# Hidden activations of one token tile kept on chip instead of passing through DRAM, in a fused attention and FFN kernel

## The chip, the core and the metric

The kernel runs on one core of a Trainium2 chip. The metric is the device time of one execution in microseconds, the median of several runs. Engines are named as in the profile: PE multiplies matrices (PEld loads its stationary operand), DVE and ACT work on vectors, POOL is the third such engine, SP issues the DMAs.

## The reference

Windowed attention over 8 x 8 heads of 576 tokens, 64 wide, then a gated feed-forward network over the 4608 tokens. All data are float32.

```
scores = q @ k^T / 8, kept where 0 <= i - j < 64
attn   = softmax(scores) @ v                  # (8, 8, 576, 64)
x      = attn, heads side by side             # (4608, 512)
out    = (sigmoid(x @ w_gate) * (x @ w_val)) @ w_out     # 512 -> 1536 -> 512
```

## The kernel before

**Tiles.** The 4608 tokens are cut into 12 tiles of TT = 384, worked off in pairs (tiles 0 and 1 are the first pair). The attention of a tile consists of four units (t, p), each two heads: scores `s` on PE (L219), softmax on DVE and ACT (L243 to L268), transposes `pp` on PE (L300), their copies `pT` on ACT (L305), the products `oo` on PE (L329), and a copy `xf` out of PSUM on ACT (L317), which makes its bank free for the next unit's scores.

**The FFN of the first pair** is done plainly. The 1536 hidden columns are NF = 12 blocks j of 128. `up` (L360) makes the gate's and the value's products of a block, `gate_table` (L369) the sigmoid, `up_val` their product `h32` (L388), and `hidden_split` (L377) splits it into a high part `hh` (L380) and a rest `hl` (L382), since a product is made of three matmuls: high by high, high by rest, rest by high. `down` (L416) multiplies these with w_out and sums over j in the PSUM tiles `y`; after the last j, ACT copies `y` to `yo` (L419), and SP stores it (L420). Tile 0 runs `down` right behind its `up`. Tile 1 runs `down` only after all blocks of both tiles are made; its blocks 0 to 9 go out to the DRAM tensor `hd` by `put_hidden` (L395, L396) and come back by `get_hidden` (L403) as `hb`; the last KEEP = 2 blocks stay in the ring of `hh` and `hl`. The later pairs run another scheme with sums and differences (products `pr`, `y` at L612), from 200 us on.

**What runs beside it.** The weights arrive as 64-bit floats and are converted in the first 190 us, 36 tiles `m_j` of 128 x 512 (m: gate, value, output): ACT makes `w32` (L117) and `raw` (L118) from a loaded tile, DVE combines them (L126, L128, L130), ACT casts the high part `w` (L157), DVE makes the rest (L158), SP stores all of it for the later pairs. Between these stand the attention units of tiles 2 and 3, and from 170 us on the preparation of the second pair: `x_prep` (L590: differences t1 and xf, L566, L567, L574) and `x_part`, `x_rest` (x_T, x_B; L602, L607), and sums of weights `ws` (L546 on ACT, L548 on DVE).

**Memory.** A tile gets a slot by its tag; several tiles with one tag take the slots in turn, and a new tile waits until the last reader of the old one is done. x0 to x13 hold the split inputs, x10 to x13 first the v of units (0,2) to (1,1); e0 to e4 are for hidden tiles of later pairs; the tag `raw` has RAW = 6 slots, the tag `w32` W32 = 3 (the conversion's w32, then yo and t1).

**Order.** Each step is put into a list `events` with a time written by hand; the list is sorted, and the steps are issued in that order to a scheduler which simulates the engines and decides in which order DVE, ACT, POOL and SP run their instructions. PE keeps the order of the program. On the chip each engine runs its instructions strictly in the order decided.

Of the kernel before, what the change touches and what calls it, by code (L numbers as in the profile page):

```python
# [9 lines left out]
F32 = mybir.dt.float32  # L10
F32R = mybir.dt.float32r
# [7 lines left out]
P = 128  # L19
BLK = 64  # L20
TT = 384
# [5 lines left out]
def attn_ffn(ctx: ExitStack, tc: tile.TileContext, qT, kT, vN, w_gate, w_val, w_out, out, outT):  # L27
# [3 lines left out]
    nc = tc.nc  # L31
# [3 lines left out]
    NF = w_gate.shape[0]  # L35
# [10 lines left out]
    RAW, W32 = 6, 3  # L46
# [3 lines left out]
    xp = ctx.enter_context(tc.tile_pool(name="xp", bufs=1))  # L50
    mp = ctx.enter_context(tc.tile_pool(name="mp", bufs=2))
    ap = ctx.enter_context(tc.tile_pool(name="ap", bufs=1))
    sm = ctx.enter_context(tc.tile_pool(name="sm", bufs=8))
    dr = ctx.enter_context(tc.tile_pool(name="dr", bufs=1, space=bass.MemoryType.DRAM))
# [286 lines left out]

    hh = {}
    yb = {}
    hd = dr.tile([NF, P, 2, TT], F32, name="hd")
    nbank = [-1]

    def h_bank(nm):
# [27 lines left out]
        gate_table(t, j, up(t, j, 0))  # L375

    def hidden_split(t, j, h32, eng):  # L377
        h_hi = mp.tile([P, TT], F32R, name=f"hh_{t}_{j}", tag="hh", bufs=3)
        h_lo = mp.tile([P, TT], F32R, name=f"hl_{t}_{j}", tag="hl", bufs=3)
        nc.vector.tensor_copy(out=h_hi, in_=h32)  # L380
        hh[(t, j)] = (h_hi, h_lo)
        return eng.tensor_sub(out=h_lo, in0=h32, in1=h_hi.bitcast(F32))  # L382

    def up_val(t, j):
        ph = up(t, j, 1)
        g = gates.pop((t, j))
        h32 = mp.tile([P, TT], F32, name=f"h32_{t}_{j}", tag="c", bufs=CB)
        nc.vector.tensor_mul(out=h32, in0=ph, in1=g)  # L388
        last = hidden_split(t, j, h32, nc.vector)
        if t == 0:  # L390
            marks[j] = (chain[-1], last.ins)

    def put_hidden(t, j):
        h_hi, h_lo = hh.pop((t, j))
        nc.sync.dma_start(out=hd[j, :, 0, :], in_=h_hi.bitcast(F32))  # L395
        nc.sync.dma_start(out=hd[j, :, 1, :], in_=h_lo.bitcast(F32))  # L396

    def get_hidden(t, j):
        if j > 5:
            hb = xp.tile([P, 2, TT], F32R, name=f"hb_{t}_{j}", tag=f"x{10 + (j + 2) % 4}")  # L400
        else:
            hb = mp.tile([P, 2, TT], F32R, name=f"hb_{t}_{j}", tag="raw", bufs=RAW)
        nc.sync.dma_start(out=hb.bitcast(F32), in_=hd[j])  # L403
        hh[(t, j)] = (hb[:, 0, :], hb[:, 1, :])


    def down(t, j, i, first, last):
        h_hi, h_lo = hh[(t, j)]
# [369 lines left out]
    UPT, DNT, PRT = 4.2, 2.1, 1.05  # L778
    events = []

    def put(tm, o, f, *a):
        events.append((tm, o, f, a))

    KEEP = 2
    AHEAD = 2
    DPT = DNT / TB
    APT = (0.9, 0.8, 0.9, 1.5, 0)
# [11 lines left out]
    for n in range(2 * NP):  # L799
        t, p = divmod(n, NP)  # L800
# [17 lines left out]
    at, now = {}, 0.0  # L818
# [5 lines left out]
    def attend(i):  # L824
        nonlocal now
        for f, t, p, *done in fill.get(i, ()):
            if f in (0, 3):
                put(now - LOAD_AHEAD, 8, load_qk, t, p)
                put(now - LOAD_AHEAD, 8.5, load_v, t, p)
            put(now, 6, stages[f], t, p, *done)  # L830
            now += APT[f]

    for i, (kind, t, j) in enumerate(plan):
        attend(i)
        at[(kind, t, j)] = now
        if (kind, t, j) == ("up", 0, 0):
            now = -9.9
        if kind == "up":
            put(now, 9, up_gate, t, j)
            now += UPT / 2  # L840
            attend(i + 0.5)
            put(now, 9, up_val, t, j)
            if t == 1 and j < NF - KEEP:
                put(now, 9.1, put_hidden, t, j)
            now += UPT / 2
        else:
            for x in range(TB):
                put(now + x * DPT, 9, down, t, j, x, j == 0, j == NF - 1)
            now += DNT
        if (kind, t, j) == ("up", 0, 0):  # L850
            now = 0.0
    for i in range(KINDS * NF):
        j, m = divmod(i, KINDS)
# [10 lines left out]
    fill[46] = [(3, *unit(2, 0))]  # L864
    fill[47] = [(4, *unit(2, 0))]

    def last_tile(t, js, ready):


        nonlocal now  # L870
        items = [(j, x) for x in range(TB) for j in js[:2]] + [(j, x) for j in js[2:-2] for x in range(TB)]
        items += [(j, x) for x in range(TB) for j in js[-2:]]
        for n, j in enumerate(js):
            put(now + n * DNT - ready[0], 9.4, ready[1], t, j)
        for n, (j, x) in enumerate(items):
            if n % TB == 0 and t == 1:
                attend(len(plan) + n // TB)
                attend(len(plan) + n // TB + 0.5)
            put(now, 9, down, t, j, x, j == js[0], j == js[-1])
            now += DPT  # L880

    last_tile(1, list(range(NF)), (7, lambda t, j: j < NF - KEEP and get_hidden(t, j)))

# [99 lines left out]
    for _, _, f, a in events:  # L985
        if f in (conv_a, conv_b, conv_c):
            with ExitStack() as behind:
                j, m = divmod(a[0], KINDS)
# [56 lines left out]
```

## Time and profile before

| | us |
|---|---|
| median of 3 runs | 970.04 (968.94 to 970.25) |
| the profiled execution | 968.12 |
| its span in the trace | 966.3 |
| PE busy | 946.8 (98%) |
| DVE busy | 692.8 (72%) |
| ACT busy | 597.3 (62%) |
| granted clock of PE | 1.0 |

The span is the time from the first to the last recorded instruction of the profiled execution; 1.8 us lie around it. In the lines of the profile, a name before the arrow is what an instruction writes, behind it what it reads, numbers left out; a bracket at a timeline row's end gives the idle time ahead of the instruction and what ended it. Times within the span are counted from its start.

### The profile page before, as it was taken

How to read it: one execution, taken by the hardware profiler on the slowest of the kernel's cores; microseconds unless marked ns; L12 is line 12 of the kernel's file. 1: busy time of each engine (PE TensorE's matmuls, PEld its weight loads, DVE VectorE, ACT ScalarE, POOL GpSimd, SP SyncE). 2: the span in 40 equal slices, each digit the busy share in tenths (PEclk: the TensorE clock that was granted, in tenths of full speed). 3: DMA queues.
4: the chain of work that ended last, by engine and by line, in shares of the span. 5: the costliest groups of instructions: out<-in, count | busy, mean ns of one | idle time of the engine just before them, and what ended most of it. 6: DMA issues, size and time to landing. Idle time of an engine off the chain costs nothing.

```text
span 966.3 us, 20552 instructions
## 1 busy us (share of the span) xinstructions
PE 946.8 (98%) x7200; PEld 904.1 (94%) x7200; DVE 692.8 (72%) x1873; ACT 597.3 (62%) x1479; POOL 141.8 (15%) x232
## 2 busy tenths in 40 slices
PE   6899999999999999999999999999999999999998
PEld 4798999889999999999999999999999999999998
DVE  7889989756776964666876666796566697567782
ACT  7888877647787644666754666664666675222350
POOL 4200103327661000110100111100110100000000
PEclk9999999999999999999999999999999999999999
DMA  9899999948998868889989888878888868988464
GB/s 344 313 384 356 398 353 346 395 165 290 319 305 283 287 205 265 279 259 323 342 265 301 285 257 271 262 258 284 293 264 259 262 212 263 306 252 257 142 211 160
DMA packets 110838, 272.41 MB, mean 282 GB/s; under 512 B 12048, under 2 KB 42896, under 8 KB 110736
## 3 DMA queue, kind: packets, MB, share of 16 engines
q1 hardware_dynamic: 110736, 271.11, 83.2%
q8 instruction: 57, 0.93, 0.4%
q14 instruction: 45, 0.37, 0.1%
HBM read 214.17 MB, written 56.89 MB: 280 GB/s over the span
## 4 chain that ended last, share of the span: by engine, by line
PE 82%; ACT 6%; DVE 5%; DMA 3%; issue 2%; POOL 1%; SPq 0%; DVEq 0%; ACTq 0%
PE pr L612 39%; PE y L612 23%; PE ph L360 6%; PE y L416 4%; PE s L219 3%; PE pp L300 2%; PE s L329 2%; ACT p L251 2%; DMA a<-w32d 1%; DMA w32d<-w 1%; PE oo L329 1%; ACT L251 1%; ACT pT L305 1%; PE pr L329 1%; ACT L369 1%
## 5 line engine op out<-in xcount | busy, mean ns | idle before, releaser
L612 PE MATMUL pr<-x_T,wt 128*128 128x384 f32 x1224 | 227.9, 338 | 0.0
L612 PEld LDWEIGHTS pr<-x_T,wt 128*128 128x128 f32 x1224 | 211.3, 188 | 4.2 <-issue 2.6
L612 PE MATMUL pr<-x_B,wt 128*128 128x384 f32 x1008 | 187.5, 336 | 0.0
L612 PE MATMUL y<-h,wot 128*128 128x384 f32 x1008 | 176.0, 334 | 0.0
L612 PEld LDWEIGHTS pr<-x_B,wt 128*128 128x128 f32 x1008 | 175.0, 188 | 0.6 <-DMA wt<-wd 0.3
L612 PEld LDWEIGHTS y<-h,wot 128*128 128x128 f32 x1008 | 174.6, 188 | 0.5 <-DVE h L655 0.3
L268 POOL TENSOR_TENSOR p<-p,rs 128x384 f32<-128x384 f32 x76 | 66.4, 888 | 567.5 <-DVE rs L259 511.2
L720 ACT CAST h<-h 128x384 fp32r<-128x384 f32 x168 | 82.6, 515 | 67.2 <-PE y L612 34.4
L251 ACT ACTIVATE p<-p,mn 128x128 f32<-128x128 f32 x288 | 111.0, 394 | 6.2 <-DVE mn L243 5.6
L360 PE MATMUL ph<-x,w 128*128 128x384 f32 x576 | 106.2, 338 | 0.1
L721 DVE TENSOR_TENSOR h<-h,h 128x384 fp32r<-128x384 f32 x168 | 88.6, 553 | 24.1 <-ACT h L720 22.7
L360 PEld LDWEIGHTS ph<-x,w 128*128 128x128 f32 x576 | 99.7, 188 | 2.4 <-issue 0.9
L243 DVE CUSTOM_DVE_ANT_0 p<-s,m 128x128 f32<-128x128 f32 x288 | 65.7, 286 | 38.8 <-PE s L219 38.5
L369 ACT ACTIVATE g<-c 128x384 f32<-128x384 f32 x90 | 46.6, 524 | 69.1 <-DVE c L651 68.8
L655 DVE TENSOR_TENSOR h<-c,g 128x384 f32<-128x384 f32 x90 | 55.9, 621 | 29.8 <-ACT g L369 25.5
L369 ACT ACT_TABLE_LOAD x40 | 51.3, 1283 | 13.4 <-DVE c L651 12.8
L305 ACT COPY pT<-pp 128x384 f32<-128x384 f32 x96 | 41.4, 480 | 28.2 <-PE pp L300 28.1
L219 PE MATMUL s<-k,q 64*64 64x128 f32 x1152 | 46.0, 287 | 7.7 <-DMA k<-in_kT_dram 4.9
L622 DVE TENSOR_TENSOR c<-pr,p 128x384 f32<-128x384 f32 x60 | 33.1, 551 | 27.7 <-PE pr L612 27.7
L251 ACT ACT_TABLE_LOAD x39 | 50.0, 1283 | 0.7
L251 ACT ACTIVATION_READ_ACCUMULATOR p<-p,mn 128x1 f32 x264 | 49.9, 189 | 0.0
L219 PEld LDWEIGHTS s<-k,q 64*64 64x64 f32 x1152 | 33.4, 138 | 14.3 <-DMA q<-in_qT_dram 5.2
(113 smaller groups left out, 1326.8 us busy)
## 6 DMA issues: line engine op xcount, KB each, us to landing
wt<-wd SPq DMA_DIRECT2D x186, 512.0 KB, 4.5
wot<-wod SPq DMA_DIRECT2D x84, 512.0 KB, 4.4
v<-in_vN_dram SPq DMA_DIRECT2D x48, 384.0 KB, 5.2
wd<-ws SPq DMA_DIRECT2D x48, 256.0 KB, 4.7
k<-in_kT_dram SPq DMA_DIRECT2D x48, 224.0 KB, 5.2
q<-in_qT_dram SPq DMA_DIRECT2D x48, 192.0 KB, 5.0
w32d<-w SPq DMA_DIRECT2D x36, 256.0 KB, 5.2
wd<-w SPq DMA_DIRECT2D x36, 256.0 KB, 5.6
```

Source lines behind the costliest of these rows:

```text
L219: pe(nc.tensor.matmul(sc[h][half * BLK:(half + 1) * BLK, u, :], qt[h * BLK:(h + 1) * BLK, U * BLK:(U + 1) * BLK], kt[h * BLK:(h + 1) * BLK ...
L243: nc.vector.tensor_tensor_reduce(out=pt[:, u, :], in0=sc[:, u, :], in1=masks[key], op0=ALU.add, op1=ALU.min, scale=-SCALE, scalar=3.0e38, ...
L251: exp = nc.scalar.activation(pt[:, u, :], pt[:, u, :], AF.Exp, bias=mn[:, u:u + 1], scale=-1.0, **sums)
L268: eng.tensor_mul(out=pt, in0=pt, in1=rs.unsqueeze(2).broadcast_to([P, UP, P]))
L305: cp = nc.scalar.copy(pT, pp)
L329: pe(nc.tensor.matmul(oo[U // 2][h * BLK:(h + 1) * BLK, U % 2 * BLK:(U % 2 + 1) * BLK], vt[:, U, h * BLK:(h + 1) * BLK], pT[h][:, U // 2, ...
L360: pe(nc.tensor.matmul(ph, l, r, start=i == 0, stop=i == len(prs) - 1))
L369: act = nc.scalar.activation(g, c, AF.Sigmoid)
L612: pe(nc.tensor.matmul(ps, l, r, start=first and i == 0, stop=last and i == 2, skip_group_check=not check))
L655: nc.vector.tensor_mul(out=hidden(s, k)[2 * r + b], in0=c, in1=gates.pop((t, j)))
L720: nc.scalar.copy(h2[:, 0, :], src)
L721: nc.vector.tensor_sub(out=h2[:, 1, :], in0=src, in1=h2[:, 0, :].bitcast(F32))
```

## The change

The ten blocks j = 0 to 9 of tile 1 are split directly into tiles `h2_1_j` that keep both parts: blocks 0 to 3 in the slots x10 to x13, 4 to 8 in e0 to e4, 9 in one slot of `raw`. `down` reads them there. `put_hidden`, `get_hidden`, the DRAM tensor `hd` and their events are gone.

```diff
-    hd = dr.tile([NF, P, 2, TT], F32, name="hd")
+    KEEP = 2
...
     def hidden_split(t, j, h32, eng):
-        h_hi = mp.tile([P, TT], F32R, name=f"hh_{t}_{j}", tag="hh", bufs=3)
-        h_lo = mp.tile([P, TT], F32R, name=f"hl_{t}_{j}", tag="hl", bufs=3)
+        if t == 1 and j < NF - KEEP:
+            pool, tag, bufs = (xp, f"x{10 + j}", 1) if j < 4 else (xp, f"e{j - 4}", 1) if j < 9 else (mp, "raw", RAW)
+            h2 = pool.tile([P, 2, TT], F32R, name=f"h2_{t}_{j}", tag=tag, bufs=bufs)
+            h_hi, h_lo = h2[:, 0, :], h2[:, 1, :]
+        else:
+            h_hi = mp.tile([P, TT], F32R, name=f"hh_{t}_{j}", tag="hh", bufs=3)
+            h_lo = mp.tile([P, TT], F32R, name=f"hl_{t}_{j}", tag="hl", bufs=3)
         nc.vector.tensor_copy(out=h_hi, in_=h32)
...
-    def put_hidden(t, j):
-        h_hi, h_lo = hh.pop((t, j))
-        nc.sync.dma_start(out=hd[j, :, 0, :], in_=h_hi.bitcast(F32))
-        nc.sync.dma_start(out=hd[j, :, 1, :], in_=h_lo.bitcast(F32))
-
-    def get_hidden(t, j):
-        if j > 5:
-            hb = xp.tile([P, 2, TT], F32R, name=f"hb_{t}_{j}", tag=f"x{10 + (j + 2) % 4}")
-        else:
-            hb = mp.tile([P, 2, TT], F32R, name=f"hb_{t}_{j}", tag="raw", bufs=RAW)
-        nc.sync.dma_start(out=hb.bitcast(F32), in_=hd[j])
-        hh[(t, j)] = (hb[:, 0, :], hb[:, 1, :])
...
-            if t == 1 and j < NF - KEEP:
-                put(now, 9.1, put_hidden, t, j)
...
-    def last_tile(t, js, ready):
+    def last_tile(t, js):
...
-        for n, j in enumerate(js):
-            put(now + n * DNT - ready[0], 9.4, ready[1], t, j)
...
-    last_tile(1, list(range(NF)), (7, lambda t, j: j < NF - KEEP and get_hidden(t, j)))
+    last_tile(1, list(range(NF)))
```

PE's order is the same but for names. With 30 DMAs less in its simulation, the scheduler orders DVE and ACT anew between about 50 and 212 us. In the kernel after, lines of `hidden_split` and `up_val` have numbers higher by 5, and those behind them lower by 9 (L557 for L566). Three places follow; each row is an instruction with its line, its output, its input and the output's size, and the last number of a name is a running number of the tile.

The first place is on ACT at 73 us, around the copy `xf_2_0` that frees the bank for the scores of unit (2,2). Before:

```order
L305 COPY pT1_2_0_1241<-pp1_2_0_1237 128x384
L117 ACTIVATE w32_1_4_1258<-raw_1_4_1182 128x512
L369 ACTIVATE g_0_3_1256<-ph0_0_3_1243 128x384
L118 ACTIVATE raw_0_5_1363<-raw_0_5_1363 128x512
L157 CAST w0_4_1265<-w32_0_4_1228 128x2x256
L118 ACTIVATE raw_1_5_1374<-raw_1_5_1374 128x512
L317 COPY xf_2_0_1316<-oo_2_0_1303 128x384
L157 CAST w1_4_1297<-w32_1_4_1258 128x2x256
L117 ACTIVATE w32_2_3_1271<-raw_2_3_1199 128x512
L118 ACTIVATE raw_2_4_1391<-raw_2_4_1391 128x512
```

The same stretch of ACT after:

```order
L305 COPY pT1_2_0_1231<-pp1_2_0_1227 128x384
L157 CAST w0_4_1255<-w32_0_4_1218 128x2x256
L369 ACTIVATE g_0_3_1246<-ph0_0_3_1233 128x384
L118 ACTIVATE raw_0_5_1353<-raw_0_5_1353 128x512
L118 ACTIVATE raw_1_5_1364<-raw_1_5_1364 128x512
L117 ACTIVATE w32_2_3_1261<-raw_2_3_1192 128x512
L157 CAST w1_4_1287<-w32_1_4_1248 128x2x256
L118 ACTIVATE raw_2_4_1381<-raw_2_4_1381 128x512
L317 COPY xf_2_0_1306<-oo_2_0_1293 128x384
```

The copy stood behind raw_1_5 and now stands behind w32_2_3, the cast w1_4 and raw_2_4 as well.

The second place is on ACT at 161 us, around the copies pT of unit (2,3). Before:

```order
L369 ACTIVATE g_1_9_2394<-ph0_1_9_2381 128x384
L157 CAST w2_8_2178<-w32_2_9_2302 128x512
L369 ACTIVATE g_0_10_2435<-ph0_0_10_2422 128x384
L117 ACTIVATE w32_0_11_2419<-raw_0_11_2365 128x512
L305 COPY pT0_2_3_2490<-pp0_2_3_2486 128x384
L305 COPY pT1_2_3_2496<-pp1_2_3_2492 128x384
```

After:

```order
L369 ACTIVATE g_1_9_2366<-ph0_1_9_2353 128x384
L157 CAST w1_11_2450<-w32_1_11_2406 128x2x256
L369 ACTIVATE g_0_10_2404<-ph0_0_10_2391 128x384
L157 CAST w2_10_2471<-w32_2_10_2418 128x512
L117 ACTIVATE w32_2_11_2591<-raw_2_11_2514 128x512
L118 ACTIVATE raw_2_11_2514<-raw_2_11_2514 128x512
L537 CAST ws0_0_0_2806<-sw_0_0_2626 128x2x256
L305 COPY pT0_2_3_2459<-pp0_2_3_2455 128x384
L537 CAST ws2_0_0_2812<-sw_0_0_2626 128x2x256
L305 COPY pT1_2_3_2465<-pp1_2_3_2461 128x384
```

The conversions are about one weight tile further ahead, and casts of the weight sums stand between the copies.

The third place is on DVE at 183 us, around the softmax of unit (3,3), whose first instruction is the ISA row with `p0_3_3` and `s0_3_3`. Before:

```order
L607 TENSOR_TENSOR x_B11_1_1_2996<-xf_2_1_2262,x_B11_1_1_2996 128x384
L388 TENSOR_TENSOR h32_1_11_2705<-ph1_1_11_2692,g_1_11_2688 128x384
L607 TENSOR_TENSOR x_B21_1_1_3057<-xf_2_3_2528,x_B21_1_1_3057 128x384
L380 CAST hh_1_11_2707<-h32_1_11_2705 128x384
L382 TENSOR_TENSOR hl_1_11_2708<-h32_1_11_2705,hh_1_11_2707 128x384
L243 ISA p0_3_3_2780,mn0_3_3_2781<-s0_3_3_2766,m_10_82 128x128
```

After:

```order
L385 CAST hh_1_11_2674<-h32_1_11_2672 128x384
L387 TENSOR_TENSOR hl_1_11_2675<-h32_1_11_2672,hh_1_11_2674 128x384
L557 TENSOR_TENSOR t1_1_0_2821<-xf_3_0_1741,xf_2_0_1306 128x384
L558 TENSOR_TENSOR xf_3_0_1741<-xf_3_2_2007,xf_3_0_1741 128x384
L565 TENSOR_TENSOR xf_2_0_1306<-xf_3_2_2007,t1_1_0_2821 128x384
L557 TENSOR_TENSOR t1_1_1_2935<-xf_3_1_2725,xf_2_1_2234 128x384
L598 TENSOR_TENSOR x_T1_1_0_2857<-t1_1_0_2821,x_T1_1_0_2857 128x384
L243 ISA p0_3_3_2741,mn0_3_3_2742<-s0_3_3_2727,m_10_82 128x128
```

The differences of `x_prep` and one `x_rest` (L566, L567, L574, L607 before) stood behind the whole softmax and now stand ahead of it.

More of the change, by code (lines that the diff above doesn't have):

```diff
@@ L782, in put @@
         events.append((tm, o, f, a))
-    KEEP = 2
     AHEAD = 2
```

## The prediction

> **What bounds the kernel now.** I read the page's busy times and the chain that ended last first, then the busy times by stretch, the waits, and at the places where the change moves something the timeline of single instructions.
>
> ```profile
> span 966.3 us, 20552 instructions
> PE 946.8 (98%) x7200; PEld 904.1 (94%) x7200; DVE 692.8 (72%) x1873; ACT 597.3 (62%) x1479; POOL 141.8 (15%) x232
> PE 82%; ACT 6%; DVE 5%; DMA 3%; issue 2%; POOL 1%; SPq 0%; DVEq 0%; ACTq 0%
> ...
> core 0: us, PE busy (x) PEld busy (x) DVE busy (x) ACT busy (x) POOL busy (x), PEclk, DMA share, GB/s
> 0.00:10.00 10.00, 5.12 (x75) 4.18 (x75) 4.18 (x32) 4.53 (x16) 3.54 (x14) 1.00 0.81 270
> 60.00:100.00 40.00, 38.54 (x287) 35.52 (x286) 36.20 (x95) 34.75 (x82) 5.66 (x6) 1.00 1.02 371
> 100.00:180.00 80.00, 80.00 (x595) 74.06 (x594) 71.88 (x178) 62.31 (x138) 20.86 (x30) 1.00 1.02 369
> 180.00:220.00 40.00, 39.78 (x271) 33.32 (x270) 21.02 (x63) 20.44 (x58) 5.17 (x8) 1.00 0.69 251
> 220.00:262.00 42.00, 40.57 (x346) 38.38 (x346) 30.31 (x87) 31.79 (x81) 29.80 (x63) 1.00 0.89 303
> ```
>
> The matmul engine is busy 98% of the span. The change touches the first pair, 48 to 210 us. There the DMA engines stand at a share of 1.0 until 180, and yet PE is full: it lacks 40.00 − 38.54 = 1.46 us in the first stretch, nothing in the second, 0.22 and 1.43 in the last two. Those 3.11 us are all that the stage has to give, whatever is taken from the DMA queues. What PE waits for in 60 to 262 us:
>
> ```profile
> PE s L219 <- ACT xf L317: 1.6, 3, 1.0
> PE s L329 <- ACT pT L305: 0.6, 1, 0.6
> PE pr L612 <- DVE ws L548: 0.6, 1, 0.6
> ```
>
> None is a DMA: ACT and DVE release PE, and on these two engines the conversion of the weights (L117, L118, L157 on ACT; L126 to L130, L158 on DVE) shares a strict order with the small copies that PE needs. So the change is costed by what it does to those two orders.
>
> **The transfers removed.** 20 writes of 192 KB and 10 reads of 384 KB, 7,680 KB or 7.86 MB.
>
> ```profile
> hb<-hd SPq DMA_DIRECT2D x10, 384.0 KB, 5.7
> hd<-hh SPq DMA_DIRECT2D x10, 192.0 KB, 5.6
> ...
> L395 SPq DMA_DIRECT2D hd<-hh x10: 382/469/943, 47.7 to 160.1; - x10
> L403 SPq DMA_DIRECT2D hb<-hd x10: 319/450/892, 134.2 to 182.0; - x10
>   PEld s L219: 0.2, 1
> ```
>
> The last row is the whole list of who waited for them: one weight load, 0.2 us, of a unit's scores behind the matmuls that read hb. SP is spared 30 issues, but nothing on PE hung on them: between −0.2 and 0, I take **0**. [...]
>
> The hidden tiles themselves are made by the same two DVE instructions, in other memory, and PE's order is the same row for row but for names: **0**. The slots are empty when wanted:
>
> ```profile
> L329 PE MATMUL oo<-pT,v x192: 222/222/270, 11.9 to 41.0; 128*64 128x64 f32 x192
> L720 ACT CAST h_p<-h x24: 497/514/542, 247.8 to 334.3; 128x384 fp32r<-128x384 f32 x24
> ```
>
> The v tiles in x10 to x13 are last read by 41.2, the first h tile comes at 247.8.
>
> **First place, 73 us: a copy falls behind three conversions.** PE's scores of unit (2,2) need the memory bank that COPY xf_2_0 (L317) empties. Before, it runs right behind raw_1_5 (L118). After, the order has w32_2_3 (L117), CAST w1_4 (L157) and raw_2_4 (L118) ahead of it, and that cast waits for DVE's L130 of w1_4.
>
> ```profile
> 72.83 0.69 ACT L118 ACTIVATE raw<-raw 128x512 int32<-128x512 uint32 x1
> 73.41 0.46 ACT L317 COPY xf<-oo 128x384 f32<-128x384 f32 x1
> 75.04 0.62 ACT L157 CAST w<-w 128x512 fp32r<-128x512 f32 x1 [1.17 <-DVE w L130]
> 75.57 0.67 ACT L117 ACTIVATE w<-raw 128x512 f32<-128x512 f32 x1
> 76.14 0.66 ACT L118 ACTIVATE raw<-raw 128x512 int32<-128x512 uint32 x1
> ...
> 74.32 0.69 DVE L130 CUSTOM_DVE_ANT_0 w<-raw,w 128x1024 uint16<-128x1024 uint16 x1
> ...
> 73.92 0.88 PE L219 MATMUL s<-k,q 64*64 64x128 f32 x22 [0.35 <-ACT xf L317]
> ```
>
> By start-to-start distances a cast takes 75.57 − 75.04 = 0.53, an L117 0.57, an L118 73.41 − 72.83 = 0.58 (the printed durations overlap). L130 ends at 75.01; so cast at 75.04, raw_2_4 at 75.57, the copy from 76.15 to 76.61, and PE goes on at 76.66 in place of 73.92: **+2.7**. Were the cast's data there already, only the work counts: 0.53 + 0.57 + 0.58 = +1.7. One more DVE conversion ahead of L130 (0.69) makes +3.4. I take +2.7, since the row shows ACT waiting for exactly that L130. On PE nothing is queued to cover it: the order is fixed, and the down matmuls stand behind these scores.
>
> **92 us.** The copy xf_2_2 has three more conversions ahead of it too (two L117, one cast: 1.67).
>
> ```profile
> 92.87 0.88 PE L219 MATMUL s<-k,q 64*64 64x128 f32 x22 [1.00 <-ACT xf L317]
> ```
>
> PE arrives 2.7 late and waited 1.00 there already; 1.67 of work fits into that lateness: between −0.3 and +0.6, I take **0**.
>
> **Second place, 163 us.** COPY pT1_2_3 has nine more ACT rows ahead of it in all: three L117, one L118, three L157 and two weight-sum casts L537 (546 before), 3 × 0.57 + 0.58 + 5 × 0.53 = 4.9 us.
>
> ```profile
> 160.97 0.86 ACT L305 COPY pT<-pp 128x384 f32<-128x384 f32 x2 [1.24 <-PE pp L300]
> 163.26 0.92 PE L329 MATMUL oo<-pT,v 128*64 128x64 f32 x24
> ```
>
> The copies end at 161.83, PE uses them at 163.26: slack 1.43. With 2.7 of lateness, 4.9 − 1.43 − 2.7 = +0.8 if ACT never idles, 0 if its wait of 1.24 here takes the surplus, +2.2 if the three casts wait 0.47 each for L130. I take **+0.4**, halfway between the first two, since that wait lies just ahead of these copies.
>
> **Third place, 183 to 196 us: the next stage's preparation ahead of a softmax.** The differences t1, xf and x_T of the next pair (L557, L558, L565, L598) now stand on DVE ahead of unit (3,3)'s softmax, five rows before its first instruction and four more inside it; and t1_1_0 lies in the slot of yo_0_0, so it waits for that output's store to land.
>
> ```profile
> 185.21 0.29 DVE L243 CUSTOM_DVE_ANT_0 p<-s,m 128x128 f32<-128x128 f32 x1 [1.31 <-PE s L219]
> 188.42 0.56 DVE L268 TENSOR_TENSOR p<-p,rs 128x384 f32<-128x384 f32 x1
> 195.20 0.56 DVE L566 TENSOR_TENSOR t<-xf,xf 128x384 f32<-128x384 f32 x1 [6.23 <-DMA out_dram<-yo]
> 196.27 0.55 DVE L574 TENSOR_TENSOR xf<-xf,t 128x384 f32<-128x384 f32 x1
> ...
> 182.36 1.09 ACT L419 COPY yo<-y 128x512 f32<-128x512 f32 x2
> ...
> 193.42 0.82 PE L300 MATMUL pp<-ident,p 128*128 128x128 f32 x6
> ...
> L420 SPq DMA_DIRECT2D out_dram<-yo x6: 337/340/699, 188.1 to 213.9; - x6
> DMA to landing us min/median/max: 2.0/4.2/7.0
> ```
>
> Before, the DVE wait of 6.23 lies behind the softmax, where PE doesn't see it. PE's transposes want p1_3_3 at 193.42, it is done at 188.98: slack 4.44. After (times without the lateness, which moves all of them): yo_0_0 is copied by about 182.9 and, with SP's queue shorter, stored from about 183.2; it lands at 185.2, 187.4 or 190.2 by the three latencies. Five rows of 0.53 (196.27 − 195.20 for two) then put the softmax's first DVE row at 187.9, 190.1 or 192.9 instead of 185.21; the four others cost 2.1 less the idle time of about 0.5 in the softmax. That makes p1 later by 4.3, 6.5 or 9.3 and PE by 0, +2.1 or +4.9. With fewer transfers in the queue, I take a landing between the first two, about 3.8: **+1.7**, bounds 0 and +4.9.
>
> **Waits that shrink.** The three waits quoted first total 2.8; at 184 (0.2), 234 (0.6) and 251 (0.6) a late PE gives others time. Their sources hang on PE themselves, so mostly they move along: −2.4 to 0, I take **−0.4**, two thirds of the one that waits for the weight sums, which are made earlier now.
>
> **Sum.** 2.7 + 0 + 0.4 + 1.7 − 0.4 = +4.4 us. The profiled execution took 968.12 (span 966.3 and 1.8 around it): 972.5. It stands 1.9 below the median of 970.04, so against the median **974.4 us**.
>
> **Rivals.** *Nothing comes of it.* The first stall is real, but PE's lateness is paid back where it waits anyway (1.0 at 92.87 and the 1.4 after 184), while the second and third place stay inside their slacks: +2.7 − 2.4 = +0.3, 970.3. For it: slacks of 1.43 and 4.44 are there. Against it: those waits hang on PE's own earlier work.
>
> *Faster: the freed DMA time brings the conversions forward.* Its place is CAST w1_4 at 75.04; with the transfers at a share of 1.02, earlier raw loads could start L117 and so L130 earlier. It decides when L130 ends 1.6 us earlier than 75.01, by 73.4: then the conversions ahead of the copy are done before PE needs it, no stall appears, and the stage gives back up to 3.11: 966.9. Against it: ten pairs of writes from 47.7 to 160.1 are 12.5 apart, so only three pairs fall before 73 us, and DVE is busy 36.20 of 40 in that stretch, so L130 is limited by DVE's order more than by loads.
>
> *More.* yo_0_0's store takes 7.0 as before (+3.2 over the forecast), or the second place costs its +2.2: 976 to 979, at 977.6.
>
> *The clock drops.* [...] The row of 0 to 10 us has PE busy 5.12 with a clock of 1.00, and there it waits 3.9 at a stretch:
>
> ```profile
> PE s L219 <- DMA k<-in_kT_dram: 4.9, 2, 3.9
> ```
>
> A longer idle stretch than 2.7, and no drop. [...]
>
> *The change does not do what it says:* a slot still in use makes DVE wait and PE with it, or the order is undone at run time. The slot rows above exclude the first, the engines' fixed orders the second; it would be no change, 970.
>
> **How the numbers follow.** A measurement of this kernel tells about 0.2%, 1.9 us: below 968.1 counts as faster, above 972.0 as slower. Forecast (first stall real and at least partly kept, 972 to 977): 0.59. More: 0.14. Clock: 0.03. Together slower 0.76. Nothing comes of it 0.15, and 0.01 that the change is none: same 0.16. Faster 0.08. The range leaves out the faster case and the upper end of "more": 969.5 to 979.0. The forecast's own range is 972 to 977.
>
> **What would show it.** First place: a wait `s` for `xf` of 2 to 3 us near 76, and nothing like it if I am wrong. Second: `oo` waiting for `pT` by under 2 us near 166. Third: the DVE wait for yo's store ahead of unit (3,3)'s softmax, then PE's `pp` waiting for DVE near 197. No row hd, and the DMA share in 100 to 180 below 1.0. After 262 us both kernels should run in step. I am wrong if the L130 of w1_4 ends early, if conversions running ahead make SP's loads of q and k for unit (3,3), now queued behind more weight stores, come too late, or if PE catches up before 262.

## The result: 1.05% slower, more than twice the loss forecast

The changed kernel takes 979.11 us (median of 4, 978.86 to 981.81) against 969.49 for the one before: ratio 1.0105, 95% interval 1.0085 to 1.0125, so 9.6 us slower. The forecast was 974.4, a loss of 4.4. The profiled execution took 979.19 us with a span of 977.4, 11.1 more than the span before.

The page after, in the lines that answer to those of before:

```profile
span 977.4 us, 20468 instructions
PE 952.3 (97%) x7200; PEld 908.5 (93%) x7200; DVE 691.8 (71%) x1873; ACT 597.7 (61%) x1479; POOL 139.8 (14%) x232
PE 79%; ACT 7%; DVE 5%; DMA 5%; issue 2%; POOL 1%; SPq 0%; DVEq 0%; ACTq 0%; POOLq 0%
```

DVE and ACT do the same work as before. In the chain PE has 3 points less, DMA 2 more, although 7.86 MB of transfers are gone. By stretch (columns as in the prediction):

```profile
60.00:100.00 40.00, 36.30 (x267) 33.24 (x266) 35.21 (x92) 32.14 (x71) 4.05 (x4) 0.96 1.02 364
100.00:180.00 80.00, 77.50 (x579) 71.46 (x578) 67.34 (x174) 62.57 (x145) 24.30 (x37) 1.00 0.88 305
180.00:220.00 40.00, 39.78 (x267) 33.05 (x266) 21.95 (x68) 20.81 (x54) 2.53 (x4) 1.00 0.46 156
220.00:262.00 42.00, 38.65 (x294) 36.49 (x292) 26.66 (x64) 25.59 (x63) 25.69 (x56) 0.96 0.84 277
```

The DMA share fell as it should, from 1.02 to 0.88 in 100 to 180. PE, which had no gap there, now lacks 2.5 us; it lacks 3.7 in the first row and 3.35 in the last; and the granted clock, 1.00 everywhere before, is 0.96 in two of the rows. PE's waits in 60 to 262:

```profile
PE s L219 <- ACT xf L317: 3.9, 3, 2.9
PE pr L603 <- DVE c L642: 2.7, 1, 2.7
PE oo L329 <- ACT pT L305: 2.5, 2, 1.9
```

PE's order is the same in both kernels, so the start of one and the same matmul in the two traces gives PE's lateness at that place. Rows of PE after:

```profile
76.46 1.55 PE L219 MATMUL s<-k,q 64*64 64x128 f32 x22 [2.88 <-ACT xf L317]
96.34 0.88 PE L219 MATMUL s<-k,q 64*64 64x128 f32 x22 [0.81 <-ACT xf L317]
169.00 0.33 PE L329 MATMUL oo<-pT,v 128*64 128x64 f32 x2 [1.92 <-ACT pT L305]
169.89 0.91 PE L329 MATMUL oo<-pT,v 128*64 128x64 f32 x22 [0.57 <-ACT pT L305]
199.92 0.82 PE L300 MATMUL pp<-ident,p 128*128 128x128 f32 x6
256.08 1.35 PE L603 MATMUL pr<-x_B,ws 128*128 128x384 f32 x6 [2.69 <-DVE c L642]
```

| matmul | before | after | lateness | what was added |
|---|---|---|---|---|
| scores of (2,2) | 73.92 | 76.46 | +2.5 | wait for copy xf_2_0 |
| first ph behind them | 76.91 | 80.96 | +4.05 | +1.5, clock at half |
| scores of (3,0) | 92.87 | 96.34 | +3.5 | 0.6 paid back, 0.4 of it by 85 and 0.2 at 92 |
| ph behind oo of (2,3) | 164.10 | 170.74 | +6.6 | +0.3 by 163, then +2.9, wait for copies pT_2_3 |
| pp of (3,3) | 193.42 | 199.92 | +6.5 | nothing |
| pp at 247.69 | 247.69 | 257.30 | +9.6 | +3.1, wait for DVE's c |
| s at 264.89 | 264.89 | 275.26 | +10.4 | +1.6, clock at half, less 0.9 paid back at 251 (time of before) |

The last 0.5, up to 10.9 at the end, comes in steps later in the kernel.

**The first place** went as forecast. ACT after:

```profile
74.85 0.62 ACT L157 CAST w<-w 128x512 fp32r<-128x512 f32 x1 [0.19 <-DVE w L130]
75.38 0.68 ACT L118 ACTIVATE raw<-raw 128x512 int32<-128x512 uint32 x1
75.95 0.46 ACT L317 COPY xf<-oo 128x384 f32<-128x384 f32 x1
```

But then the clock fell. Single microseconds of the same trace:

```profile
74.00:75.00 1.00, 0.00 (x0) 0.00 (x0) 1.00 (x3) 0.81 (x3) 0.00 (x0) 1.00 0.96 306
77.00:78.00 1.00, 1.00 (x19) 0.67 (x11) 1.00 (x3) 0.00 (x0) 0.00 (x0) 0.50 1.11 313
80.00:81.00 1.00, 1.00 (x6) 0.79 (x5) 0.97 (x2) 0.99 (x6) 0.00 (x0) 1.00 0.88 246
```

After a gap of 2.88 us the clock (third column from the end) is 0.50 for about 3.4 us. PE is called busy there, so the busy time hides the loss; the clock column, the lateness and the length of the rows show it: 22 matmuls of scores take 1.55 us at 76.46 and 0.88 at 96.34.

**The second place** cost more than its rows. ACT stood idle twice between 162 and 167: 2.40 us for an L130 of DVE, and 0.95 for the load of raw_2_11. That load on SP, in the first row before, in the others after, with the L130 and what ACT made of both:

```profile
149.88 0.43 SPq L105 DMA_DIRECT2D raw<-in_moe_w_out_dram  x1
...
162.72 0.32 SPq L446 DMA_DIRECT2D wd<-w  x1
163.09 0.44 SPq L105 DMA_DIRECT2D raw<-in_moe_w_out_dram  x1
...
164.55 0.68 DVE L130 CUSTOM_DVE_ANT_0 w<-raw,w 128x1024 uint16<-128x1024 uint16 x1
...
165.26 0.62 ACT L157 CAST w<-w 128x512 fp32r<-128x512 f32 x1 [2.40 <-DVE w L130]
166.84 0.67 ACT L117 ACTIVATE w<-raw 128x512 f32<-128x512 f32 x1 [0.95 <-DMA raw<-in_moe_w_out_dram]
```

The larger wait is DVE's: from 155 to 169 it waits for nothing, and this L130 stands behind other conversion rows and ends at 165.23. The smaller one is SP's: the scheduler had put the load behind three weight stores that wait for DVE, so it left 13.2 us later than before, and ACT's conversion of that tile waited for it. The copies pT stood behind both.

**The third place** happened and cost nothing here: the store of yo_0_0 landed 3.3 us after its issue, the differences started at 191.99, and p1_3_3 was done at 199.71 instead of 188.98. Less PE's lateness of 6.5 that is 4.2 later, just inside the slack of 4.44: `pp` started at 199.92 and waited for nothing.

```profile
191.99 0.56 DVE L557 TENSOR_TENSOR t<-xf,xf 128x384 f32<-128x384 f32 x1 [3.11 <-DMA out_dram<-yo]
...
198.69 1.02 DVE L268 TENSOR_TENSOR p<-p,rs 128x384 f32<-128x384 f32 x2
```

**A fourth place** was not foreseen, near 256 us. Rows after; the last two are the same instructions before:

```profile
246.90 0.62 ACT L537 CAST ws<-sw 128x512 fp32r<-128x512 f32 x1 [2.95 <-DMA wd<-ws]
251.78 3.77 DVE L258 SCALAR_TENSOR_TENSOR rs<-rs 128x6 f32<-128x6 f32 x1 [1.65 <-ACT p L251]
254.66 0.87 POOL L529 TENSOR_TENSOR sw<-a,sw 128x128 f32<-128x128 f32 x2
...
238.22 0.62 ACT L546 CAST ws<-sw 128x512 fp32r<-128x512 f32 x1 [0.83 <-DMA wd<-ws]
243.60 0.24 DVE L258 SCALAR_TENSOR_TENSOR rs<-rs 128x6 f32<-128x6 f32 x1 [1.36 <-ACT p L251]
```

A cast waits 2.95 instead of 0.83 for a store to land; the softmax behind it reaches DVE while POOL runs sums without a break; and a row of DVE that takes 0.24 lasts 3.77, until 0.02 us after POOL's run ends at 255.53. PE's bank stands behind it on DVE.

### The profile page after: what moved, and what is told of

Its sections match the earlier page's. It is cut to its first block, busy times and chain, and to the rows that moved or that the text cites. A ratio compares the mean times of both kernels' runs of the same rounds, so it can differ in the third digit from the quotient of the medians.

```text
span 977.4 us, 20468 instructions
## 1 busy us (share of the span) xinstructions
PE 952.3 (97%) x7200; PEld 908.5 (93%) x7200; DVE 691.8 (71%) x1873; ACT 597.7 (61%) x1479; POOL 139.8 (14%) x232
## 4 chain that ended last, share of the span: by engine, by line
PE 79%; ACT 7%; DVE 5%; DMA 5%; issue 2%; POOL 1%; SPq 0%; DVEq 0%; ACTq 0%; POOLq 0%
PE pr L603 37%; PE y L603 23%; PE ph L360 6%; PE y L407 4%; PE s L219 3%; ACT p L251 2%; PE pp L300 2%; PE s L329 2%; ACT L251 1%; DMA w32d<-w 1%; PE oo L329 1%; ACT g L369 1%; ACT L369 1%; ACT pT L305 1%; DMA raw<-in_moe_w_val_dram 1%
## 5 line engine op out<-in xcount | busy, mean ns | idle before, releaser
L268 POOL TENSOR_TENSOR p<-p,rs 128x384 f32<-128x384 f32 x76 | 66.0, 883 | 571.6 <-DVE rs L259 560.1
```

The source lines that it names most:

```text
L268: eng.tensor_mul(out=pt, in0=pt, in1=rs.unsqueeze(2).broadcast_to([P, UP, P]))
```

## The experiments

Most of them hold an engine to a chosen order. `ORDER` lists, for an engine, the instructions (numbered as the code issues them) in the order wanted; each is queued behind the one ahead of it, with no wait added:

```diff
+    for eng, ranks in ORDER.items():
+        t = [i for i in nc.cur_bb.bb.instructions if str(i.engine).endswith(eng)
+             and type(i).__name__ not in ("BassTilePoolBoundary", "InstRegisterMove")]
+        for a, b in zip(ranks, ranks[1:]):
+            tc.add_manual_dep(t[b], t[a].name,
+                              mybir.DependencyInfo(mybir.DependencyClass.NoSync, mybir.DependencyReason.DATA),
+                              reason="order")
```

SP's order stays with the scheduler. The times:

| kernel | us | ratio to before (95%) | stalls / ramp of the profiled run |
|---|---|---|---|
| the change | 979.11 | 1.0105 (1.0085 to 1.0125) | 7.8 / 3.1 |
| e1 order of before | 970.47 | 1.0009 (0.9998 to 1.0019) | 1.9 / 0.4 |
| e2 first place repaired | 979.16 | 1.0106 (1.0091 to 1.0120) | 7.3 / 1.9 |
| e3 second place repaired | 978.67 | 1.0101 (1.0087 to 1.0114) | 6.6 / 3.2 |
| e9 both | 977.95 | 1.0089 (1.0074 to 1.0104) | 6.9 / 1.0 |
| e13 three places | 975.46 | 1.0068 (1.0055 to 1.0080) | 5.4 / 2.3 |
| e14 five places | 976.19 | 1.0077 (1.0063 to 1.0091) | 5.8 / 0.8 |
| e10 halfway | 978.89 | 1.0097 (1.0081 to 1.0112) | 7.0 / 2.4 |
| e5 early part old | 979.30 | 1.0100 (1.0085 to 1.0115) | 8.5 / 3.0 |
| e6 late part old | 976.13 | 1.0087 (1.0062 to 1.0112) | 8.1 / 4.3 |
| e8 late part old, POOL not | 980.39 | 1.0119 (1.0105 to 1.0132) | 6.5 / 4.2 |
| e7 POOL old | 979.95 | 1.0101 (1.0085 to 1.0117) | 6.8 / 5.4 |
| e11 AHEAD = 1 | 983.81 | 1.0153 (1.0138 to 1.0167) | 12.9 / 4.4 |
| e4 before, copy behind 3 | 973.41 | 1.0045 (1.0033 to 1.0057) | 4.4 / 2.1 |
| e12 before, copy behind 1 | 971.83 | 1.0020 (1.0009 to 1.0031) | 1.5 / 1.0 |

The last column takes PE's lateness against the trace of before from 44 us on: steps of over 0.25 us between neighbouring matmuls are counted as stalls, less such steps back; the rest is ramp, which is mostly time at a halved clock (e9 and e14, whose clock stays at 1.00 from 44 us on, have 1.0 and 0.8 of it). It is for one execution; the ramp differs from one execution to the next. e6 ran from 975.0 to 982.5: its two long executions, the profiled one of 981.5 among them, have a mean granted clock of 0.992 and 0.991, the four short ones 0.996 to 1.000.

**e1: is it the order?** The changed kernel with the order of before on ACT, DVE and POOL.

> The changed kernel (hidden tiles on chip, no transfers) with ACT, DVE and POOL held to the order that the kernel before has. Theory O (the new orders on ACT and DVE cost the time, the memory places and the missing transfers cost nothing): no long stalls at 76, 169 and 256, about 970, between 967 (all 3.1 of the stage's PE gaps given back) and 970.5. Rival M (the places or the changed DMA traffic disturb the stage, whatever the order): it stays at 977 to 980.

```profile
100.00:180.00 80.00, 80.00 (x594) 74.10 (x593) 71.57 (x178) 63.20 (x137) 20.93 (x31) 1.00 0.92 317
```

970.47, no different from before: its interval allows a loss of up to 1.8 us, against 9.6 for the change. So the loss is in the order of the rows, and at most 1.8 of it in the places in memory. And with the order equal the 30 transfers saved bring nothing, though the DMA share falls to 0.92: PE is full (80.00 of 80) with and without them.

**e4 and e12: the first stall alone, in the kernel before.** Only copy xf_2_0 moves, behind three rows or one:

```diff
 ACTIVATE raw_1_5
-COPY xf_2_0
 CAST w1_4
+COPY xf_2_0        (e12)
 ACTIVATE w32_2_3
 ACTIVATE raw_2_4
+COPY xf_2_0        (e4)
```

> The kernel before, transfers and all, in its own orders but for one row on ACT: COPY xf_2_0 behind cast w1_4, w32_2_3 and raw_2_4. Theory O: PE waits about 2.7 more at 74, the gap is about 3.1, the granted clock falls for about 3 us (another 1.5), 0.5 comes back at 92: 970.0 + 3.7 = 973.7. Without a drop of the clock: 972.2. Rival (the stall needs the new traffic or places): 970.

> The kernel before with copy xf_2_0 behind cast w1_4 alone: the gap of PE at 74 should be about 2.2 to 2.5, where the three rows made 4.0 and a drop of the clock. If the clock drops only after gaps above 2.6: +2.0 less 0.6 paid back at 92, 969.3 + 1.5 = 970.8, clock 1.00 in 70 to 90. If it drops here too: +1.5 more, 972.3.

```profile
70.00:80.00 10.00, 5.99 (x64) 5.00 (x63) 8.41 (x23) 7.67 (x15) 0.00 (x0) 0.81 1.01 346
80.00:90.00 10.00, 10.00 (x48) 9.23 (x48) 7.96 (x24) 6.43 (x20) 1.80 (x2) 0.85 1.02 373
```

Both rows are e4's: the clock, third column from the end, is 0.81 and 0.85, which is 6.8 us at 0.50. e4 loses 4.1 by the medians; in its trace, one of its longer executions, there are a gap of 4.0 us (a lateness of 3.7), 2.5 of ramp, 1.2 paid back by 93, and 1.0 more at 251. e12 loses 2.5: 1.7 of wait, 1.4 of ramp behind a gap of 2.02, 1.2 paid back by 93, 0.6 again at 251. So e4's moved copy costs what was forecast for it (973.7), the drop of the clock belongs to it, and in e12's profiled execution half the gap didn't spare it.

**e2, e3, e9: repairs of single places** in the changed order, on ACT alone:

```diff
 e2, e9
+COPY xf_2_0
 ACTIVATE w32_2_3
 CAST w1_4
 ACTIVATE raw_2_4
-COPY xf_2_0
 e3, e9
 ACTIVATE g_0_10
+COPY pT0_2_3
+COPY pT1_2_3
 CAST w2_10
...
-COPY pT0_2_3
 CAST ws2_0_0
-COPY pT1_2_3
+COPY xf_2_3
 CAST w2_10
-COPY xf_2_3
```

> The changed kernel in its own orders but for one row on ACT: COPY xf_2_0 back ahead of w32_2_3, cast w1_4 and raw_2_4. Theory O with its parts additive: the stall of 2.5 at 76 and the drop of the clock behind it (1.5) both go, clock 1.00 in 70 to 80, 979.1 - 4.0 = 975.1. Rival A (later stalls hang on ACT, DVE and DMA alone): what PE gains here it waits longer at 169, 978 to 979.

> The changed kernel in its own orders but for ACT near 165 us: the copies pT of unit (2,3) ahead of the cast w2_10, w32_2_11, raw_2_11 and the two sum casts, and copy xf_2_3 ahead of the second cast w2_10. Theory O: the wait of oo for pT (2.3 and 0.8) goes, 979.1 - 3.0 = 976.1, and the stall at 256 stays. Rival: the conversions pushed back make the weight sums late, and the same 3 come back at 240 to 260, 979.

> The changed kernel in its own orders but with both repairs on ACT: copy xf_2_0 first at 73 us, and copies pT of (2,3) and xf_2_3 first at 165 us. Theory A (stalls add up): 979.1 - 4.0 - 3.0 = 972. Theory L (what counts is the lead: how many conversion rows stand ahead of PE's rows that did not before, up to 11 on DVE and 9 on ACT between 73 and 180 us; PE must come late by their work, at whichever row): DVE's lead is untouched, so 978 to 980, with the waits at other rows, on DVE's products above all.

No gain from either, and 1.2 us from both; all three differences to 979.11 are within the intervals. PE's waits in 60 to 300 us, of e2 (first three), e3 (next two) and e9:

```profile
PE s L219 <- ACT xf L317: 2.7, 4, 1.5
PE oo L329 <- ACT pT L305: 2.4, 2, 1.9
PE ph L360 <- ACT g L369: 1.5, 1, 1.5
...
PE s L219 <- ACT xf L317: 4.6, 4, 3.4
PE pp L300 <- DVE p L268: 1.8, 2, 1.5
...
PE pp L300 <- DVE p L268: 1.9, 1, 1.9
PE ph L360 <- ACT g L369: 1.8, 2, 1.5
```

With the first stall gone, PE waits for the gate g_1_3 at 84 (1.5) and longer at 95; with the second gone, the third place shows: pp waits for DVE's p by 1.5 to 1.9. A stall repaired uncovers the next, which had been hidden behind the lateness. Plain adding of stalls, 972 for e9, is refuted. The times of e2 and e3 are those of their rivals, but not at the places that these named: e2 waits at 84 and 95, e3 at 200. e9 stands at the lower edge of Theory L's 978 to 980, but its longest waits are for ACT and for DVE's softmax, and none is for DVE's products.

**e13, e14: three and five places.** e13 also puts the nine rows t1, xf, x_T on DVE behind the softmax of (3,3), and the four casts x_T on ACT behind its exponentials; e14 also puts g_1_3 ahead of w32_1_5 and copy xf_2_2 ahead of cast w0_6.

```diff
 e13, DVE
-TENSOR_TENSOR t1_1_0
-TENSOR_TENSOR xf_3_0
...
 ISA p0_3_3
...
 TENSOR_TENSOR p1_3_3
+TENSOR_TENSOR t1_1_0
+TENSOR_TENSOR xf_3_0
...
 e14, ACT
+ACTIVATE g_1_3
 ACTIVATE w32_1_5
 CAST w0_5
-ACTIVATE g_1_3
...
+COPY xf_2_2
 CAST w0_6
 ACTIVATE w32_1_6
-COPY xf_2_2
```

> As the kernel with both repairs on ACT, and the third place repaired too: on DVE the nine rows t1, xf, x_T behind the softmax of unit (3,3), on ACT its four casts x_T behind the exponentials. Separate places, the next hidden behind the last: the wait of 1.9 at 197 (PE pp for DVE p) goes, 978.0 - 2.1 = 975.9. A fixed lateness demanded by the order as a whole: 977 to 979, the 2 us back at 235 to 260.

> Two more repairs on ACT: the gate g_1_3 ahead of w32_1_5 and the cast w0_5, and copy xf_2_2 ahead of the cast w0_6 and w32_1_6. Separate places: the waits of PE near 84 (1.5 for g) and 95 (1.5, of which 1.0 were there before) shrink too, 975.9 - 1.9 - 0.5 = 973.5. A fixed lateness: 977 to 979.

e13 gains about 2 us on e9 (2.5 by the medians, 2.0 by the ratios, whose intervals still touch), as separate places would have it, and is clear of the change's interval; no row of pp waiting for p is left. e14 gains nothing more and fits neither of its forecasts. Its first two windows:

```profile
60.00:100.00 40.00, 37.24 (x278) 34.03 (x277) 34.63 (x89) 31.04 (x70) 4.05 (x4) 1.00 1.00 358
100.00:180.00 80.00, 77.50 (x576) 70.87 (x576) 67.63 (x175) 62.14 (x142) 22.46 (x34) 1.00 0.87 307
```

and the chain by line, in 78 to 100 us, of e14 and of before (the view ends its lines there):

```profile
by line: issue 13.1%; DVE w L130 12.4%; ACT L251 11.7%; DVE w L158 11.5%; ACT p L251 10.4%; DVE w L128 9.7%; ACT w L157 8.5%; ACT L369 5.8%; DVE zz L126 5.7%; DVE h L393 4.7%; ACT w L117 2.5%; DVE hl L387 2.5%; DVE h L387 2.5%; ACT g L369 2
...
by line: PE ph L360 28.6%; issue 12.1%; ACT p L251 10.7%; DVE w L130 9.5%; DVE w L128 6.1%; ACT L251 5.8%; DVE zz L126 4.2%; PE s L219 4.0%; ACT pT L305 3.9%; DVE rs L258 3.5%; DVE w L158 3.4%; ACT w L117 2.7%; DVE hl L382 2.5%; ACT w L157 
```

Before, PE's products lead that chain; in e14 no PE is named, and the four costliest entries of DVE are rows of the conversion. PE's stalls are now short (1.2 at most), the clock stays at 1.00, and 5.8 us of stalls are left all the same. That points at DVE's row order, which e14 keeps but for nine rows; no run shows it.

**e5 to e8: which part.** e5 has the order of before up to copy xf_2_3, e6 behind it; e8 is e6 with POOL left in the changed order; e7 changes POOL alone, from 200 us on.

```diff
 POOL, e6 and e7 (near 250 us)
+TENSOR_TENSOR ws0_0_2
+TENSOR_TENSOR ws2_0_2
 TENSOR_TENSOR sw_0_3
-TENSOR_TENSOR ws0_0_2
-TENSOR_TENSOR ws2_0_2
```

> The changed kernel with the order of before on ACT, DVE and POOL up to copy xf_2_3 (about 165 us), and its own orders from there. Theory A (the stalls add up): only what comes after 165 us is left of the lateness, 10.9 - 6.5 = 4.4, so 970.5 + 4.4 = 974 to 975. Theory R (each place of the changed order demands a lateness of its own, and PE's total is the largest of them, not their sum): the last place, near 250 us, demands all of it by itself, 978 to 979.

> The reverse: its own orders up to copy xf_2_3, then the order of before on ACT, DVE and POOL. Both theories: the lateness stands at 6.5 behind 165 us and nothing is added at 250, about 976 (970.5 + 6, less what waits absorb). Rival: the lateness comes from the first part alone and grows to the 10.9 whatever the later order, 979.

> The changed kernel with its own orders on ACT and DVE; POOL alone has the order of before from 200 us on (the weight sums ws made ahead of the next sums sw). If POOL's order makes the stall at 256 us (2.9, and 1.4 by the clock): 979.1 - 4.3 = 974.8. If ACT's and DVE's order makes it: 979.

> As the kernel with the late order of before, but POOL keeps the changed order: only ACT and DVE have the order of before behind copy xf_2_3. If POOL's order makes the stall at 256 us: it stays, 979. If ACT's and DVE's does: about 976, as with all three.

e5 settles nothing. Its 979.30 is close to Theory R's 978 to 979, but the stall near 250 us that this needs isn't there (no wait over 1.2 behind 250); joining the two orders made a wait of its own at 181.7.

```profile
PE ph L360 <- DVE h L393: 4.3, 1, 4.3
```

e6 comes out at its 976 by the median, though its interval reaches to that of the change. In e7 the stall of 2.7 at 256 is gone, but the kernel isn't faster: 5.4 us of ramp in its profiled run make up for it. And the stall is gone in e2, e3, e8, e9 and e14 too, which keep POOL's changed order, and back in e13 (2.5). e8's 980.39 is near the 979 of its first forecast, but without the stall that this forecast kept. So POOL's order is not shown to be the cause of the stall; where it appears, DVE's row meets a long run of POOL (the row takes 3.77 us after, 3.42 in e13), and what decides that is open.

**e10 and e11: dose, and a simple remedy.** e10 puts each row halfway between its two places. e11 is one line:

```diff
-    AHEAD = 2
+    AHEAD = 1
```

> The changed kernel with each row of ACT, DVE and POOL halfway between its place in the order of before and in its own: the lead falls from 9 to 5 rows on ACT and from 11 to 7 on DVE. Theory L: the lateness falls to about half, 970.5 + 5 = 974 to 976. Theory A: the two named stalls stay or go one by one; copy xf_2_0 still has two conversions ahead of it (2.0 and perhaps the clock), pT1_2_3 five: 972 to 979, no number of its own. If only the full order of before is good: 979.

> The changed kernel with one number changed, AHEAD = 1 for 2: the conversions of gate and value weights of block j are queued behind the steps of block j-1 and not j-2. The scheduler then leads by at most 5 rows on ACT and 8 on DVE, and not at all before 90 us. Theory L: no stall at 76, about half the lateness, 973 to 976. Rival: the weights now come too late, PE's products ph wait for w, 980 or more.

Theory L failed in both. Half the lead of the conversions costs nearly all of the loss (7.0 of stalls), so the loss isn't in proportion to it; 978.89 is the 979 forecast for the case that only the full order of before is good. Holding the conversions back by a block is worse, as the rival of e11 said (980 or more), though not by products ph waiting for w: copies pT come late, products wait for a gate, and `down` for weights.

```profile
PE oo L329 <- ACT pT L305: 3.5, 3, 2.9
PE ph L360 <- ACT g L369: 3.2, 3, 2.2
PE y L407 <- DVE w L158: 1.0, 1, 1.0
```

No kernel tried here beats the one before.

## Why the prediction was right in sign and wrong in size

In PE's lateness, the sum of the profiled execution reads: 2.5 at the first place, +1.5 by the clock, −0.6 paid back by 93 us, +0.3 by 163, +2.9 at the second place, −0.1 at 184, 0 at the third place, +3.1 at 256, +1.6 by the clock, −0.9 paid back at 251 (time of before), +0.5 later. That is 10.9 before rounding, where the forecast was 4.4. Three steps make the difference: the clock, the second place, and the stretch behind 196 us.

- *What bounds the kernel, and the removed transfers at 0*: right. e1 has them removed and the order kept, and is no faster.
- *First place, +2.7*: right, 2.5; e4 and e12 show the mechanism in the kernel before.
- *The clock*, a rival with 0.03: wrong. It came after two gaps, +1.5 and +1.6. The step that failed is the reading of the row of 0 to 10 us as proof that a wait of 3.9 leaves the clock at 1.00. The trace of before holds no record of the clock ahead of 10.6 us, and the profile counts 1.00 where it has none. PE's rows of before contradict that 1.00: 24 matmuls of scores took 1.56 us right behind the wait of 3.9, and 24 of the same shape 0.89 later, the ratio that 0.50 and 1.00 gave in the trace after (1.55 and 0.88 for 22). The other runs show the drop after gaps of 1.9 to 4.3.

```profile
3.89 1.56 PE L219 MATMUL s<-k,q 64*64 64x128 f32 x24 [3.89 <-DMA k<-in_kT_dram]
...
11.09 0.89 PE L219 MATMUL s<-k,q 64*64 64x128 f32 x24
```

- *92 us, 0*: right, 0.2 was paid back there, inside the bounds. Another 0.4 came back ahead of it, by 85 us.
- *Second place, +0.4, bounds 0 to +2.2*: mis-sized, 2.9. The prediction counted ACT's nine rows and took waits of at most 0.47 each for L130. ACT waited 2.40 for one L130, and 0.95 for a load that SP's order had put 13.2 us later; where that load stands, the prediction didn't look.
- *Third place, +1.7*: the mechanism is real (waits of 1.5 in e3 and 1.9 in e9, and about 2 us gained in e13), but in this kernel p1 was 4.2 later and stayed within its slack of 4.44, as the lower bound said. It was close: 0.2 us more and PE would have waited.
- *Waits that shrink, −0.4*: −0.1 at 184 and −0.9 at 251 came, within the bounds; the wait for the weight sums, for which the term was taken, didn't shrink (0.6 before, 0.7 after).
- *Behind 196 us* the sum has no term but that one, and this failed too: a new wait of 2.7 came at 256, where the prediction took the work on ACT and DVE to be in step again. A store that landed 2.1 us later relative to its cast, and a DVE row that took 3.77 and ended with POOL's run, made it.
- The rival "more" comes near by its number, 977.6, but by luck: the store of yo_0_0 took 3.3 and not 7.0. Of its two conditions only the second place's +2.2 came, and was exceeded.
- The rival "nothing comes of it" is refuted, and so is "faster": the conversions did go ahead, but into a stall.

Why single repairs don't return what they seem to cost is shown in part: they uncover hidden waits (e2, e3, e9, e13). Why 5.8 us of stalls are left in e14, and half the shift costs as much as all of it, is argued from the chain on DVE and not shown; ACT's order and DVE's were not tried apart.

## What to carry to other kernels

- Removing transfers is a change to the schedule as well: where a scheduler orders engines by simulated times, compare the orders of every engine, the DMA queue and POOL included, before counting what is saved.
- In a kernel with PE at 98%, price a stall with what follows it: here gaps from 1.9 us on could halve the clock for 3.4 or 6.8 us, and that cost 1.4 to 2.5 us more in the four places where it was read.
- A stall seen is not a gain in store. Fix the order as a whole (here the old one, held by edges) rather than the row that waits.

## What the runs showed of the hardware

**The clock fell after shorter gaps than the prediction took.** Counting stretches from 11 to 300 us in which neither PE nor its weight load was busy, and the clock in the microseconds behind them: all 11 gaps between 2.5 and 4.3 us were followed by 0.50, 5 of 9 between 1.9 and 2.2, and only a few of those near 1 (the one that ended at 20.12 in e12 was, the one of 1.00 at 92.87 before was not). In the traces of before and after the time between two changes of the recorded clock is a whole number of steps of 3.413 us: one step at 0.50, and 18, 52, 210 and 280 at 1.00. In the other runs a stretch at 0.50 lasted 3.4 us, and longer once each in e4 to e8 (6.8 in e4). The shortest of the 11 gaps, in e13:

```profile
251.00:252.00 1.00, 0.00 (x0) 0.00 (x0) 1.00 (x1) 0.14 (x1) 1.00 (x4) 1.00 1.04 390
253.00:254.00 1.00, 1.00 (x3) 1.00 (x4) 1.00 (x3) 0.00 (x0) 0.00 (x0) 0.50 1.08 360
256.00:257.00 1.00, 1.00 (x9) 1.00 (x8) 1.00 (x3) 0.91 (x2) 0.00 (x0) 1.00 0.82 322
```

Gaps of 1.9 us fell on either side: the one of 1.92 that ended at 168.99 after left the clock at 1.00, the one of 1.9 that ended at 169.63 in e2 was followed by 0.50. What decides it was not shown.

**A row of DVE lasted until a run of POOL ended.** L258, a row of 0.17 us by its median, took 1.46 at 229.76 in the trace before, 3.77 in the one after and 3.42 in e13, each time ending 0.02 to 0.03 us after POOL's last instruction of an unbroken run. In e13:

```profile
248.96 3.42 DVE L258 SCALAR_TENSOR_TENSOR rs<-rs 128x6 f32<-128x6 f32 x1 [1.65 <-ACT p L251]
251.47 0.88 POOL L529 TENSOR_TENSOR sw<-a,sw 128x128 f32<-128x128 f32 x2
```

A single row of POOL did the same: before, L258 at 13.36 took 0.66 and ended 0.02 us behind the row L268 that POOL had begun at 13.18. In the three longer cases the row lasted until the whole run had ended and not for one instruction of 0.44 us; it isn't certain either, since the row at 243.60 before took 0.24 with POOL at work. The cause was not shown.
